# Two column groups by two token blocks in seven block products instead of eight, and four phases, in the second feed-forward network

## The chip, the cores and the metric

The kernel runs on one core of a Trainium2 chip. A core has engines that work at the same time, each through its own queue in order: TensorE (PE, matmuls; PEld are its weight loads), VectorE (DVE), ScalarE (ACT), GpSimd (POOL) and SyncE (SP), which here issues the DMAs. The metric is the device time of one execution in microseconds (us); 1 us is 1000 ns.

## The reference

```python
def reference(...):
    attn_out = _attn_ref(...)                     # 2 x 8 heads, 768 tokens, depth 64, a window of 128 and 4 sinks
    x = attn_out.transpose(0, 2, 1, 3).reshape(1536, 512)
    x = ((x @ w_a) * (x @ w_b)) @ w_out           # first network: d_ff 1536
    h = np.maximum(x @ w_in, 0.0)                 # second network: d_ff 2048
    return (h * h) @ w_out2
```

All of it is in float32. The change lies in `x @ w_in`, the second network's first product: 1536 tokens, depth 512, 2048 columns.

## The kernel before

**Data.** Activations lie with the depth on the 128 partitions: `xh` and `xl` hold four slices of depth by 1536 tokens. Each float32 number is split into a rounded high half and the rest (`split`, lines 59 and 60: ScalarE casts the high half, VectorE subtracts for the low half). A product takes three matmuls per slice of depth: high by high, high by low, low by high.

**Weights.** They come from DRAM as 64-bit words, in pieces of 128 x 512 numbers (a column group's first-product weights for all four slices of depth, or its second-product weights). SyncE loads a piece into one of three `wraw` buffers. `Weights.stages` decodes it: ScalarE takes the upper words (line 517), VectorE runs four operations (521, 522, 525, 528), ScalarE casts the high half `wh` (533), VectorE subtracts the low half `wl` (535). The two halves fill a slot; there are 14 slots `FIRST` and 9 more (`NSLOT`, pool `sb`) from the end of the attention. `ahead` is called at every beat of the network's program and decodes the next piece at every third beat (`PACE`) if a slot is free; `done` gives a phase's slots back after the last token block.

**Loops.** The tokens are three blocks of 512, the column groups have 128 columns. A network works in phases of a few column groups: the first in (4, 4) after four groups done beside the attention, the second in (5, 5, 6). In each phase `block` runs over the three token blocks. For a column group in the second network: `inner` (line 625) runs 12 matmuls of 128x512 into one PSUM bank `psa`; ScalarE takes relu (695), VectorE squares (705), `split` makes `gh` and `gl`, and `outer` (line 666) runs 12 matmuls with the second-product weights into four accumulators `acc`, one half before and one behind the next group's `inner`. At the end of a phase the accumulators are drained into `part` (copy, line 725, in the first phase; addition, line 727, in later ones), and in the last phase stored (731). In the last phase of the first network `part` is the network's result and is split into `xh` and `xl`. PSUM has four banks for `psa` (`ps_a`) and four for `acc` (`ps_y`).

**Order.** In the attention an order written out by hand holds on TensorE, VectorE, ScalarE and GpSimd. Behind it the scheduler of the Tile framework places the instructions of all engines, by its own estimates and by the program's order; it moves matmuls of neighbouring steps into each other.

Of the kernel before, what the change touches and what calls it, by code (L numbers as in the profile page):

```python
# [18 lines left out]
P = 128  # L19
SK = 8  # L20
AHEAD1 = 4
PHASES1 = (4, 4)
PHASES2 = (5, 5, 6)
FIRST, NSLOT = 14, 9
PACE = 3
NRAW, AHEAD = 3, 2
# [14 lines left out]
T = 512  # L41
# [414 lines left out]
class Weights:  # L456
# [7 lines left out]
    def __init__(self, tc, cp, rp, w_a, w_b, w_out, w_in2, w_out2):  # L464
        self.tc, self.rp = tc, rp
        self.n = 0
        FF1, FF2 = w_a.shape[0], w_in2.shape[0]

        def piece(w, f):
            return w.bitcast(I32)[f]  # L470


        f = AHEAD1
        self.phases = [[(piece(w_a, j), piece(w_b, j)) for j in range(f)]]
        for n in PHASES1:
            self.phases.append([(piece(w_a, j), piece(w_b, j), piece(w_out, j)) for j in range(f, f + n)])
            f += n
        assert f == FF1
        self.phases[1][0:0] = [(piece(w_out, j),) for j in range(AHEAD1)]
        f = 0  # L480
        for n in PHASES2:
            self.phases.append([(piece(w_in2, j), piece(w_out2, j)) for j in range(f, f + n)])
            f += n
        assert f == FF2
        self.todo = [(ph, f, j) for ph in range(len(self.phases)) for f in range(len(self.phases[ph]))
                     for j in range(len(self.phases[ph][f]))]
        self.order = list(self.todo)
# [17 lines left out]
    def stages(self, pin=False):  # L505

        while len(self.raws) < AHEAD and self.next < len(self.order):
            self.load()
        nc = self.tc.nc
        key = self.todo.pop(0)  # L510
        hi, lo = slot = self.free.pop(0)
        self.where[key] = slot
        raw = self.raws.pop(0)
        up, low = raw[:, :, 1], raw[:, :, 0]
        t = self.rp.tile([P, 512], I32, name="wtmp", tag="wtmp", bufs=3)
        tf = t.bitcast(F32)
        a = nc.scalar.activation(tf, up.bitcast(F32), AF.Abs)  # L517
# [12 lines left out]
        while len(self.raws) < AHEAD - 1 and self.next < len(self.order):  # L530
            self.load()
        yield
        nc.scalar.copy(hi, tf)  # L533
        yield
        nc.vector.tensor_sub(lo, tf, hi.bitcast(F32))  # L535
        yield

    def convert(self):

        if not self.todo or not self.free:  # L540
# [12 lines left out]
    def get(self, ph, f, j):  # L553
        while (ph, f, j) not in self.where:
            assert self.convert()
        return self.where[ph, f, j]

    def done(self, ph, f):

        for j in range(len(self.phases[ph][f])):  # L560
            self.free.append(self.where[ph, f, j])


class Beside:
# [43 lines left out]
class Ffn:  # L608


    def __init__(self, tc, W, xh, xl, gp, out):
        self.tc, self.W, self.xh, self.xl, self.gp, self.out = tc, W, xh, xl, gp, out

        self.gs = [gp.tile([P, AHEAD1, T], F32, name=f"gs{j}", tag=f"gs{j}") for j in range(xh.shape[2] // T)]
        self.part = {}

    def inner(self, ph, f, j, ts, ps_a):
        W, xh, xl = self.W, self.xh, self.xl
# [10 lines left out]
    def ahead(self, t0, last, ps_a, wk):  # L629


        nc = self.tc.nc
        ts = slice(t0, t0 + T)
        for f in range(AHEAD1):
            u = wk.tile([P, T], F32, name="u", tag="u")
            pa = self.inner(0, f, 0, ts, ps_a)
            yield "fu"
            nc.scalar.copy(u, pa)
            yield None
            pb = self.inner(0, f, 1, ts, ps_a)  # L640
# [4 lines left out]
            yield None  # L645

    def block(self, ph, t0, last, ps_y, ps_a, wk):

# [73 lines left out]
        for j, b_ in enumerate(acc):  # L722
            p_ = self.part[blk][:, j]
            if first:
                nc.scalar.copy(p_, b_)
            else:
                nc.vector.tensor_add(p_, p_, b_)
            if final and one:
                split(nc, xh[:, j, ts], xl[:, j, ts], p_)
            elif final:  # L730
                nc.sync.dma_start(self.out[t0 + j * P:t0 + (j + 1) * P, :], p_)
        yield
# [2 lines left out]
@with_exitstack  # L735
def sliding_window_moe_kernel(ctx, tc, q, k, v, vs, span, w_a, w_b, w_out, w_in2, w_out2, out):
    nc = tc.nc
    NT, DM = out.shape
    cp = ctx.enter_context(tc.tile_pool(name="cp", bufs=1))
    xp = ctx.enter_context(tc.tile_pool(name="xp", bufs=1))  # L740
    xh = xp.tile([P, DM // P, NT], F32R, name="xh")
    xl = xp.tile([P, DM // P, NT], F32R, name="xl")
    rp = ctx.enter_context(tc.tile_pool(name="rp", bufs=3))
    sa = ctx.enter_context(tc.tile_pool(name="sa", bufs=1))

    def slots(pool, n):
        return [(pool.tile([P, 512], F32R, name=f"wh{j}"), pool.tile([P, 512], F32R, name=f"wl{j}")) for j in range(n)]

    first = slots(sa, FIRST)
    zero = cp.tile([P, P], mybir.dt.bfloat16, name="zero")  # L750
    nc.vector.memset(zero, 0.0)
    mk = ctx.enter_context(ExitStack())
    tp = mk.enter_context(tc.tile_pool(name="mk", bufs=1, side="right"))
    c = setup(tc, cp, tp, span)

    def run(attend):
        W = Weights(tc, cp, rp, w_a, w_b, w_out, w_in2, w_out2)
        W.free = list(first)
        F = Ffn(tc, W, xh, xl, xp, out)
        with ExitStack() as c0:  # L760
            c0.callback(mk.close)
            wk0 = c0.enter_context(tc.tile_pool(name="wk0", bufs=2, side="right"))
            beside = Beside(tc, W, F, wk0, c0, zero, NT)
            with ExitStack() as c1, tc.manual_schedule(engines=ORDERED):
                attend(c1, beside)
            with tc.tile_pool(name="sb", bufs=1) as sb:
                W.free += slots(sb, NSLOT)
                for at in beside.work:
                    if at is None:
                        W.ahead()  # L770
                c0.close()
                with ExitStack() as c2:
                    ps_a = c2.enter_context(tc.tile_pool(name="ps_a", bufs=4, space=PSUM))
                    ps_y = c2.enter_context(tc.tile_pool(name="ps_y", bufs=4, space=PSUM))
                    wk = c2.enter_context(tc.tile_pool(name="wk", bufs=2))
                    for ph in range(1, len(W.phases)):
                        for t0 in range(0, NT, T):
                            for _ in F.block(ph, t0, t0 + T == NT, ps_y, ps_a, wk):
                                W.ahead()

    def attend_any(ctx, beside):
# [76 lines left out]
```

## Time and profile before

| what | value |
|---|---|
| time, median of 3 runs | 651.21 us (650.08 to 651.23) |
| the profiled execution's own time | 650.44 us |
| its span | 648.6 us |
| TensorE's granted clock, mean | 0.999 |
| instructions | 8803 |

The span goes from the first to the last instruction of the profiled execution; its own time also has what lies around that. A matmul's end is modelled, and its record overlaps the next one's, so counts and spacing say more than the sum of durations. The attention, with parts of the first network beside it, ends at about 126 us; the second network's first products begin among the last matmuls of the first network, and the first eviction of one (line 695) starts at 381.9 us.

### The profile page before, as it was taken

The page shows a single profiled execution, that of the slowest core. Times are in us where ns is not written, and L with a number is a line of the kernel's source. Part 1 is how long each engine was busy: PE and PEld are TensorE (multiplying, and loading weights), DVE is VectorE, ACT ScalarE, POOL GpSimd, SP SyncE. Part 2 cuts the span into 40 slices and gives each one's busy share as a digit, 9 for nine tenths or more (in the row PEclk, how much of TensorE's full clock was granted, in tenths as well). Part 3 has the DMA queues.
Part 4 walks back from the last instruction along what each step waited for, and adds up shares of the span by engine and source line. Part 5 has one row for each costly group of instructions (what it writes and reads, how often), then busy time and mean ns, then how long its engine had stood idle before and what let it go on. Part 6 is the DMA issues. An engine that isn't in the chain of part 4 may idle for free.

```text
span 648.6 us, 8803 instructions
## 1 busy us (share of the span) xinstructions
PE 636.6 (98%) x3206; PEld 515.5 (79%) x3206; DVE 385.7 (59%) x908; ACT 278.9 (43%) x652; POOL 56.2 (9%) x132
## 2 busy tenths in 40 slices
PE   9889999999999999999999999999999999999996
PEld 6567777887888888888888888888888888888885
DVE  6989988238889525997324998228624233232323
ACT  6898777425446225554213554326522222222221
POOL 2554354300000000000000000000000000000000
PEclk9999999999999999999999999999999999999999
DMA  8544422003444300444000243002000000010101
GB/s 295 193 134 138 168 82 74 2 33 116 144 163 162 131 0 33 158 164 165 1 1 9 89 162 114 17 0 71 28 1 1 1 1 0 1 48 18 44 23 70
DMA packets 17411, 49.47 MB, mean 76 GB/s; under 512 B 2064, under 2 KB 2576, under 8 KB 17360
## 3 DMA queue, kind: packets, MB, share of 16 engines
q1 hardware_dynamic: 17216, 48.83, 21.6%
q8 instruction: 27, 0.44, 0.3%
q14 instruction: 24, 0.20, 0.1%
q10 hardware_dynamic: 144, 0.00, 0.0%
HBM read 45.68 MB, written 3.15 MB: 75 GB/s over the span
## 4 chain that ended last, share of the span: by engine, by line
PE 93%; DVE 3%; ACT 1%; issue 1%; POOL 0%; POOLq 0%; ACTq 0%
PE psa L625 50%; PE acc L666 35%; PE x L325 3%; PE sc L226 3%; PE ptp L287 1%; PE x L330 1%; DVE ex L242 1%; ACT ex L250 1%; PE psw L352 0%; DVE wtmp L525 0%; ACT ex L265 0%; DVE wtmp L528 0%; DVE sc L239 0%; DVE wtmp L521 0%; PE pst L311 0%
## 5 line engine op out<-in xcount | busy, mean ns | idle before, releaser
L625 PE MATMUL psa<-xh,wh 128*128 128x512 f32 x480 | 188.2, 392 | 0.0
L625 PE MATMUL psa<-xh,wl 128*128 128x512 f32 x480 | 186.8, 390 | 0.0
L625 PE MATMUL psa<-xl,wh 128*128 128x512 f32 x480 | 186.8, 389 | 0.0
L625 PEld LDWEIGHTS psa<-xh,wl 128*128 128x128 f32 x480 | 90.1, 188 | 18.9
L625 PEld LDWEIGHTS psa<-xl,wh 128*128 128x128 f32 x480 | 90.2, 188 | 18.3
L625 PEld LDWEIGHTS psa<-xh,wh 128*128 128x128 f32 x480 | 90.1, 188 | 18.2
L705 DVE TENSOR_TENSOR g<-u 128x512 f32<-128x512 f32 x48 | 33.2, 691 | 112.4 <-ACT u L695 112.4
L695 ACT ACTIVATE u<-psa 128x512 f32<-128x512 f32 x48 | 28.7, 598 | 120.6 <-PE psa L625 120.5
L59 ACT CAST gh<-g 128x512 fp32r<-128x512 f32 x72 | 44.7, 621 | 69.9 <-DVE g L702 36.0
L666 PE MATMUL acc<-wh,gl 128*128 128x512 f32 x192 | 74.7, 389 | 0.0
L666 PE MATMUL acc<-wl,gh 128*128 128x512 f32 x192 | 74.7, 389 | 0.0
L60 DVE TENSOR_TENSOR gl<-g,gh 128x512 fp32r<-128x512 f32 x72 | 49.7, 690 | 31.8 <-ACT gh L59 31.6
L517 ACT ACTIVATE wtmp<-wraw 128x512 f32<-128x512 f32 x68 | 45.8, 676 | 47.1 <-DMA wraw<-in_moe_w_out_dram 9.9
L666 PE MATMUL acc<-wh,gh 128*128 128x512 f32 x192 | 62.7, 389 | 0.0
L535 DVE TENSOR_TENSOR wl<-wtmp,wh 128x512 fp32r<-128x512 f32 x68 | 47.4, 700 | 17.0 <-ACT wh L533 16.0
L533 ACT CAST wh<-wtmp 128x512 fp32r<-128x512 f32 x68 | 41.9, 619 | 36.0 <-DVE wtmp L528 15.7
L666 PE MATMUL acc<-gl,wh 128*128 128x512 f32 x144 | 56.1, 390 | 0.2 <-DVE gl L60 0.2
L666 PE MATMUL acc<-gh,wl 128*128 128x512 f32 x144 | 56.0, 389 | 0.0
L525 DVE SCALAR_TENSOR_TENSOR wtmp<-wraw,wtmp 128x512 int32<-128x512 int32 x68 | 47.0, 696 | 0.3
L666 PE MATMUL acc<-gh,wh 128*128 128x512 f32 x144 | 47.1, 389 | 0.0
L528 DVE SCALAR_TENSOR_TENSOR wtmp<-wraw,wtmp 128x512 int32<-128x512 int32 x68 | 46.3, 685 | 0.2
L666 PEld LDWEIGHTS acc<-wh,gh 128*128 128x128 f32 x192 | 36.0, 188 | 7.5
(83 smaller groups left out, 719.4 us busy)
## 6 DMA issues: line engine op xcount, KB each, us to landing
wraw<-in_moe_w_out_dram SPq DMA_DIRECT2D x28, 512.0 KB, 3.5
wraw<-in_moe_w_in_dram SPq DMA_DIRECT2D x16, 512.0 KB, 3.4
wraw<-in_moe_w_a_dram SPq DMA_DIRECT2D x12, 512.0 KB, 3.4
wraw<-in_moe_w_b_dram SPq DMA_DIRECT2D x12, 512.0 KB, 3.5
values<-in_v_dram SPq DMA_DIRECT2D x12, 256.0 KB, 4.1
out_dram<-part SPq DMA_DIRECT2D x12, 256.0 KB, 2.2
keys<-in_k_dram SPq DMA_DIRECT2D x11, 272.0 KB, 3.9
queries<-in_q_dram SPq DMA_DIRECT2D x11, 256.0 KB, 3.8
```

The source lines that it names most:

```text
L59: nc.scalar.copy(hi, src)
L60: (lo_eng or nc.vector).tensor_sub(lo, src, hi.bitcast(F32))
L226: nc.tensor.matmul(o, lhsT=half(queries[n], r)[:, 2 * m + pp], rhs=y, start=True, stop=True)
L517: a = nc.scalar.activation(tf, up.bitcast(F32), AF.Abs)
L525: nc.vector.scalar_tensor_tensor(out=t, in0=up, scalar=0x3FFFFFFF, in1=t, op0=ALU.bitwise_or, op1=ALU.bitwise_and)
L528: nc.vector.scalar_tensor_tensor(out=t, in0=low, scalar=29, in1=t, op0=ALU.logical_shift_right, op1=ALU.bitwise_or)
L533: nc.scalar.copy(hi, tf)
L535: nc.vector.tensor_sub(lo, tf, hi.bitcast(F32))
L625: self.tc.nc.tensor.matmul(ps, lhsT=w[:, kt, :], rhs=x[:, kt, ts], start=n == 0, stop=n == 3 * KT - 1)
L666: mm = nc.tensor.matmul(acc[d], lhsT=a, rhs=b_, start=f == 0 and j == 0, stop=f == NF - 1 and j == 2)
L695: nc.scalar.activation(u, pa, AF.Relu)
L705: nc.vector.tensor_mul(g, u, u)
```

## The change

The second network's first product is formed for two column groups (f, f + 1) and token blocks 0 and 1 together, in a unit. The two groups by the two halves of depth are a 2 x 2 matrix of weight blocks A, the halves of depth by the two token blocks one of activations B. Instead of eight block products (each two slices of depth, 6 matmuls) there are seven, in Winograd's form:

S1 = A21 + A22, S2 = S1 - A11, S3 = A11 - A21, S4 = A12 - S2; T1 = B12 - B11, T3 = B22 - B12, T2 = B22 - T1, T4 = B21 - T2.

C11 = A11 B11 + A12 B21. With V = A11 B11 + S2 T2 and Z = V + S3 T3: C21 = Z + A22 T4, C22 = Z + S1 T1, C12 = V + S1 T1 + S4 B22.

- `sum_x` makes the T of both slices once: 8 subtractions of 128x512 on GpSimd, in place of the `part` values of token blocks 0 and 1, each followed by a `split`; six slots taken out of the pool by `take` hold them, T1 lies in the place of B12 in `xh` and `xl`.
- `Weights.sums` makes the S of one pair: 4 GpSimd operations of 128x256 on the decoded words `wtmp` of the two pieces, then two splits into two slots. The order of a pair's pieces is now both first-product pieces, the sums, both second-product pieces; `order`, by which they are loaded, follows.
- `unit` runs the seven products. `px` keeps a running sum over five of them, which ScalarE copies out on the way; `py` has two products and `pz` one. The outputs of block 0 (C11, C21) are squared and split at once, those of block 1 are kept as squares in `ax` tiles until the accumulators of block 0 are drained. A relu and a square in one VectorE operation (line 738) take the place of two operations in three of the four outputs.
- `two` runs the two units of a phase and the second products of both blocks; block 2 runs through `block` as before.
- The phases are (4, 4, 4, 4). Nine slots become six, and three more (`early`) live only in phase 1; their room later holds the `ax` tiles.

```diff
-PHASES2 = (5, 5, 6)
+PHASES2 = (4, 4, 4, 4)
+NSUM, NAUX = 6, 3
...
+                self.todo += [(ph, f, 0), (ph, f + 1, 0), (ph, f, "sums"), (ph, f, 1), (ph, f + 1, 1)]
...
+    def sums(self, key, slot):
...
+        a11, a12, a21, a22 = a[:, 0:256], a[:, 256:512], b[:, 0:256], b[:, 256:512]
+        t, u = self.aux[0]
+        s1, s2, s3, s4 = t[:, 0:256], t[:, 256:512], u[:, 0:256], u[:, 256:512]
+        nc.gpsimd.tensor_add(s1, a21, a22)
+        nc.gpsimd.tensor_sub(s2, s1, a11)
+        nc.gpsimd.tensor_sub(s3, a11, a21)
+        nc.gpsimd.tensor_sub(s4, a12, s2)
+        yield
+        for (hi, lo), x in zip(two, (t, u)):
+            split(nc, hi, lo, x)
+        yield
...
+    def sum_x(self):
...
+        for k in range(2):
+            b11, b21, b12, b22 = b0[:, k], b0[:, 2 + k], b1[:, k], b1[:, 2 + k]
+            t1, t3, t2, t4 = b11, b12, b22, b21
+            nc.gpsimd.tensor_sub(t1, b12, b11)
+            nc.gpsimd.tensor_sub(t3, b22, b12)
+            nc.gpsimd.tensor_sub(t2, b22, t1)
+            nc.gpsimd.tensor_sub(t4, b21, t2)
+            self.sx[1, k] = xh[:, k, one], xl[:, k, one]
+            for n, t in ((1, t1), (3, t3), (2, t2), (4, t4)):
+                if n > 1:
+                    self.sx[n, k] = at.pop(0)
+                split(nc, *self.sx[n, k], t)
...
+    def unit(self, ph, f, ps_a, wk):
...
+        def add(ps, slot, n, xs, start):
+            for k in range(2):
+                hi, lo = w(slot, 2 * n + k)
+                bh, bl = xs(k)
+                for j, (a, b) in enumerate(((hi, bh), (hi, bl), (lo, bh))):
+                    nc.tensor.matmul(ps, lhsT=a, rhs=b, start=start and k == 0 and j == 0, stop=k == 1 and j == 2,
+                                     skip_group_check=True)
+
+        def square(c):
+            nc.vector.scalar_tensor_tensor(out=c, in0=c, scalar=0.0, in1=c, op0=ALU.max, op1=ALU.mult)
...
+        a0, a1 = W.get(ph, f, 0), W.get(ph, f + 1, 0)
+        sa, sb = W.get(ph, f, "sums")
+        c11 = wk.tile([P, T], F32, name="g", tag="g")
+        c12, c22 = W.aux[1 + f // 2]
+        px, py, pz = (ps_a.tile([P, T], F32, name=n, tag="ab") for n in ("px", "py", "pz"))
+        add(px, a0, 0, lambda k: x(k, first), True)
+        nc.scalar.copy(c11, px)
+        yield
+        add(pz, a0, 1, lambda k: x(2 + k, first), True)
+        nc.vector.tensor_add(c11, c11, pz)
+        square(c11)
+        yield (f, *halves(c11))
+        add(px, sa, 1, lambda k: self.sx[2, k], False)
+        nc.scalar.copy(c12, px)
+        yield
+        add(py, sa, 0, lambda k: self.sx[1, k], True)
+        yield
+        add(px, sb, 0, lambda k: self.sx[3, k], False)
+        nc.scalar.copy(c22, px)
+        nc.vector.tensor_add(c22, c22, py)
+        square(c22)
+        yield "fill"
+        add(px, a1, 1, lambda k: self.sx[4, k], False)
+        u = wk.tile([P, T], F32, name="u", tag="u")
+        nc.scalar.activation(u, px, AF.Relu)
+        nc.vector.tensor_mul(u, u, u)
+        yield "fill"
+        yield (f + 1, *halves(u))
+        add(py, sb, 1, lambda k: x(2 + k, one), False)
+        nc.vector.tensor_add(c12, c12, py)
+        square(c12)
+        self.later += [(f, c12), (f + 1, c22)]
+        W.done_sums(ph, f)
+        yield "fill"
+        yield "fill"
...
             if final and one:
-                split(nc, xh[:, j, ts], xl[:, j, ts], p_)
+                if blk != 1 or j > 1:
+                    split(nc, xh[:, j, ts], xl[:, j, ts], p_)
...
-                W.free += slots(sb, NSLOT)
+                W.free += slots(sb, NSLOT - NAUX)
...
                     for ph in range(1, len(W.phases)):
-                        for t0 in range(0, NT, T):
+                        if ph >= W.second:
+                            for _ in F.two(ph, ps_y, ps_a, wk):
+                                W.ahead()
+                        for t0 in range(2 * T if ph >= W.second else 0, NT, T):
                             for _ in F.block(ph, t0, t0 + T == NT, ps_y, ps_a, wk):
                                 W.ahead()
+                            if ph + 1 == W.second and t0 == T:
...
+                                F.sum_x()
```

Two places show how the order of the instructions moves. The first is TensorE between two column groups of the second network, whose matmuls the scheduler has moved into each other; `psa` is the bank of a group's first product, `wh` and `wl` are its weights, `acc` the second product's accumulators. Before:

```order
L625 MATMUL psa_4527<-xh_61,wh2_73 128x512
L625 MATMUL psa_4527<-xl_62,wh2_73 128x512
...
L666 MATMUL acc_4277<-wh8_1949,gh_4454 128x512
L666 MATMUL acc_4278<-wh8_1949,gh_4454 128x512
L666 MATMUL acc_4279<-wh8_1949,gh_4454 128x512
L666 MATMUL acc_4280<-wh8_1949,gh_4454 128x512
L625 MATMUL psa_4527<-xh_61,wl2_74 128x512
L625 MATMUL psa_4527<-xh_61,wh2_73 128x512
```

Of the change, the two units of the second of the four phases: `px_4321` and `px_4417` are their running banks; `wh0_69`, `wh3_1939`, `wh5_1943`, `wh2_1937` are slots that hold T3 and T2, `wh2_73` and `wh0_1933` hold weight sums.

```order
L734 MATMUL pz_4419<-xh_61,wl13_96 128x512
L734 MATMUL px_4321<-wh0_69,wh2_73 128x512
L734 MATMUL px_4321<-wl0_70,wh2_73 128x512
...
L734 MATMUL px_4321<-wh3_1939,wl2_74 128x512
L793 MATMUL acc_4316<-wh7_83,gh_4339 128x512
...
L793 MATMUL acc_4319<-wh7_83,gh_4339 128x512
L734 MATMUL px_4417<-wh5_1943,wh0_1933 128x512
...
L734 MATMUL px_4417<-wh2_1937,wl0_1934 128x512
L793 MATMUL acc_4316<-wh7_83,gl_4340 128x512
...
L793 MATMUL acc_4319<-wl7_84,gh_4339 128x512
L734 MATMUL px_4321<-wh4_1941,wh12_93 128x512
...
L734 MATMUL px_4321<-wh1_1935,wl12_94 128x512
```

Between two products of one `px` stand a product of the other unit's and second products; a group's twelve matmuls in one bank have become sixes in turn.

The second place is ScalarE in the passage from the first network to the second, from the splits of token block 1's result on; `u` are evictions of the first network's last column groups (token block 2), `part1_...` the result of token block 1. Before:

```order
L533 CAST wh1_71<-wtmp_3697 128x512
L693 COPY u_3615<-psa_3617 128x512
L517 ACTIVATE wtmp_3825<-wraw_3783 128x512
L59 CAST xh_61<-part1_2789 128x512 x2
L533 CAST wh2_73<-wtmp_3743 128x512
...
L533 CAST wh4_77<-wtmp_3825 128x512
L693 COPY u_3649<-psa_3651 128x512
L59 CAST gh_3645<-g_3616 128x512
```

Of the change (`wh0_69` to `wh1_1935` are the slots of the x sums, `wh4_77` and `wh5_79` hold pieces of weights):

```order
L60 CAST wh0_69<-part1_2792 128x512
L549 CAST wh4_77<-wtmp_3726 128x512
L884 COPY u_3592<-psa_3594 128x512
L60 CAST wh3_1939<-part1_2792 128x512
L60 CAST wh5_1943<-part1_2792 128x512
L549 CAST wh5_79<-wtmp_3766 128x512
L533 ACTIVATE wtmp_3809<-wraw_3764 128x512
L60 CAST wh2_1937<-part1_2792 128x512
L60 CAST gh_3628<-g_3593 128x512
L60 CAST wh4_1941<-part0_2475 128x512
L60 CAST wh1_1935<-part0_2475 128x512
```

Casts of x sums, which wait for GpSimd and VectorE, now stand in ScalarE's queue between the decoding of weights, the evictions and the casts `gh` of the first network's last block.

## Rows read from the trace of the kernel before

**Rows 1.** The page, part 1: busy us, share, instructions of each engine.

```profile
PE 636.6 (98%) x3206; PEld 515.5 (79%) x3206; DVE 385.7 (59%) x908; ACT 278.9 (43%) x652; POOL 56.2 (9%) x132
```

**Rows 2.** The page, part 4: the chain that ended last, by engine, by line.

```profile
PE 93%; DVE 3%; ACT 1%; issue 1%; POOL 0%; POOLq 0%; ACTq 0%
PE psa L625 50%; PE acc L666 35%; PE x L325 3%; PE sc L226 3%; PE ptp L287 1%; PE x L330 1%; DVE ex L242 1%; ACT ex L250 1%; PE psw L352 0%; DVE wtmp L525 0%; ACT ex L265 0%; DVE wtmp L528 0%; DVE sc L239 0%; DVE wtmp L521 0%; PE pst L311 0%
```

**Rows 3.** All of TensorE's waits: us in total, times, longest us.

```profile
PE pst L311 <- POOL sp L281: 4.5, 6, 1.0
PE psw L352 <- DVE zero L751: 1.0, 1, 1.0
PE sc L226 <- DVE nb L242: 0.2, 1, 0.2
PE acc L666 <- DVE gl L60: 0.2, 1, 0.2
```

**Rows 4.** Windows: length, busy (count) PE, PEld, DVE, ACT, POOL; PEclk, DMA, GB/s.

```profile
206.00:398.50 192.50, 192.50 (x851) 159.40 (x850) 126.96 (x232) 78.94 (x135) 0.00 (x0) 1.00 0.24 85
398.50:634.50 236.00, 236.00 (x1043) 195.42 (x1042) 91.87 (x146) 66.94 (x113) 0.00 (x0) 1.00 0.06 23
...
354.00:406.00 52.00, 52.00 (x231) 43.06 (x230) 47.55 (x88) 26.80 (x46) 0.00 (x0) 1.00 0.34 121
```

**Rows 5.** The page, part 5: one group of first-product matmuls.

```profile
L625 PE MATMUL psa<-xh,wh 128*128 128x512 f32 x480 | 188.2, 392 | 0.0
```

**Rows 6.** The chain in order of time: start us, us, what; two pieces.

```profile
128.04 21.85 PE psa L625 x96
...
248.09 10.88 PE acc L666 x48
```

**Rows 7.** Timeline of VectorE: start, us, engine, line, operation; three in a row.

```profile
216.00 0.68 DVE L60 TENSOR_TENSOR gl<-g,gh 128x512 fp32r<-128x512 f32 x1
216.60 0.42 DVE L521 TENSOR_SCALAR wtmp<-wtmp 128x512 f32<-128x512 f32 x1
216.94 0.68 DVE L528 SCALAR_TENSOR_TENSOR wtmp<-wraw,wtmp 128x512 int32<-128x512 int32 x1
```

**Rows 8.** ScalarE's groups by line: busy, mean ns, idle before.

```profile
L59 ACT CAST gh<-g 128x512 fp32r<-128x512 f32 x72 | 44.7, 621 | 69.9 <-DVE g L702 36.0 <-DVE g L705 33.8
...
L695 ACT ACTIVATE u<-psa 128x512 f32<-128x512 f32 x48 | 28.7, 598 | 120.6 <-PE psa L625 120.5
...
L725 ACT COPY part<-acc 128x512 f32<-128x512 f32 x24 | 12.6, 595 | 10.0 <-PE acc L666 10.0
```

**Rows 9.** GpSimd's elementwise forms: ns min/median/max; the last from its groups.

```profile
L279 POOL TENSOR_TENSOR ex<-ex,ss x20: 238/238/241, 13.2 to 118.0; 128x32 f32<-128x32 f32 x20
...
L304 POOL TENSOR_SCALAR_AFFINE_SELECT lu<-th x20: 634/635/1085, 19.9 to 125.2; 128x512 f32<-128x512 f32 x20
...
masks.py:199 POOL TENSOR_SCALAR_AFFINE_SELECT ident<-ident 128x128 f32<-128x128 f32 x1 | 0.3, 292 | 0.0
```

**Rows 10.** Timeline of GpSimd and VectorE in the attention, operations that overlap.

```profile
76.29 0.64 POOL L304 TENSOR_SCALAR_AFFINE_SELECT lu<-th 128x512 f32<-128x512 f32 x1
...
76.68 0.80 DVE L525 SCALAR_TENSOR_TENSOR wtmp<-wraw,wtmp 128x512 int32<-128x512 int32 x1
...
86.32 0.64 POOL L302 TENSOR_SCALAR_AFFINE_SELECT lu<-th 128x512 f32<-128x512 f32 x1 [1.25 <-ACT th L291]
...
86.34 0.90 DVE L522 TENSOR_SCALAR wtmp<-wtmp 128x512 int32<-128x512 int32 x1
...
98.63 1.08 POOL L304 TENSOR_SCALAR_AFFINE_SELECT lu<-th 128x512 f32<-128x512 f32 x1
```

**Rows 11.** The page, part 6: DMA loads, KB each, us to landing.

```profile
wraw<-in_moe_w_in_dram SPq DMA_DIRECT2D x16, 512.0 KB, 3.4
```

**Rows 12.** Timeline of the end: the last matmul and the last addition.

```profile
642.33 0.39 PE L666 MATMUL acc<-wl,gh 128*128 128x512 f32 x1
642.76 0.69 DVE L727 TENSOR_TENSOR part<-part,acc 128x512 f32<-128x512 f32 x1 [0.67 <-PE acc L666]
```

More of the change, by code (lines that the diff above doesn't have):

```diff
@@ L486, in __init__ @@
                      for j in range(len(self.phases[ph][f]))]
-        self.order = list(self.todo)
+        second = 1 + len(PHASES1)
+        self.todo = [key for key in self.todo if key[0] < second]
+        for ph in range(second, len(self.phases)):
+            for f in range(0, len(self.phases[ph]), 2):
+                self.todo += [(ph, f, 0), (ph, f + 1, 0), (ph, f, "sums"), (ph, f, 1), (ph, f + 1, 1)]
+        self.second = second
+        self.order = [key for key in self.todo if key[2] != "sums"]
+        self.kept = []
+        self.keep = NSUM
+        self.early, self.gone = [], []
         self.next = 0
@@ L510, in stages @@
         key = self.todo.pop(0)
-        hi, lo = slot = self.free.pop(0)
+        early = key[0] == 1 and self.early
+        hi, lo = slot = (early or self.free).pop(0)
         self.where[key] = slot
+        if key[2] == "sums":
+            yield from self.sums(key, slot)
+            return
         raw = self.raws.pop(0)
@@ L516, in stages @@
         tf = t.bitcast(F32)
+        if key[0] >= self.second and key[2] == 0:
+            self.kept.append(tf)
         a = nc.scalar.activation(tf, up.bitcast(F32), AF.Abs)
@@ L536, in stages, with take @@
         yield
-    def convert(self):
-        if not self.todo or not self.free:
+    def sums(self, key, slot):
+        nc = self.tc.nc
+        two = [slot, self.free.pop(0)]
+        self.where[key] = two
+        a, b = self.kept
+        self.kept = []
+        a11, a12, a21, a22 = a[:, 0:256], a[:, 256:512], b[:, 0:256], b[:, 256:512]
[9 more added lines that the diff above has]
+        yield
+    def take(self):
+        assert len(self.free) >= self.keep
+        got = [self.free.pop() for _ in range(self.keep)]
+        self.keep = 0
+        return got
+    def convert(self):
+        if not self.todo:
+            return False
+        ph, _, j = self.todo[0]
+        if ph == 1 and self.early:
+            pass
+        elif len(self.free) < (2 if j == "sums" else 1) + (self.keep if ph >= self.second else 0):
             return False
@@ L556, in get, with done_sums @@
         return self.where[ph, f, j]
+    def done_sums(self, ph, f):
+        self.free += self.where[ph, f, "sums"]
     def done(self, ph, f):
         for j in range(len(self.phases[ph][f])):
-            self.free.append(self.where[ph, f, j])
+            slot = self.where[ph, f, j]
+            (self.early if any(slot is x for x in self.gone) else self.free).append(slot)
 class Beside:
@@ L615, in __init__ @@
         self.part = {}
+        self.made = []
     def inner(self, ph, f, j, ts, ps_a):
@@ L645, in ahead @@
             yield None
+    def sum_x(self):
+        nc, xh, xl = self.tc.nc, self.xh, self.xl
+        at = self.W.take()
+        (b0, b1), one = (self.part[i] for i in range(2)), slice(T, 2 * T)
+        self.sx = {}
+        for k in range(2):
[10 more added lines that the diff above has]
+                split(nc, *self.sx[n, k], t)
@@ new lines, in unit, with x, w, halves @@
+    def unit(self, ph, f, ps_a, wk):
+        nc, W, xh, xl = self.tc.nc, self.W, self.xh, self.xl
+        first, one = slice(0, T), slice(T, 2 * T)
+        def x(k, ts):
+            return xh[:, k, ts], xl[:, k, ts]
+        def w(slot, k):
+            return [t[:, k * P:(k + 1) * P] for t in slot]
+        def add(ps, slot, n, xs, start):
[7 more added lines that the diff above has]
+            nc.vector.scalar_tensor_tensor(out=c, in0=c, scalar=0.0, in1=c, op0=ALU.max, op1=ALU.mult)
+        def halves(g):
+            gh = wk.tile([P, T], F32R, name="gh", tag="gh", bufs=3)
+            gl = wk.tile([P, T], F32R, name="gl", tag="gl", bufs=3)
+            split(nc, gh, gl, g)
+            return gh, gl
+        a0, a1 = W.get(ph, f, 0), W.get(ph, f + 1, 0)
[33 more added lines that the diff above has]
+        yield "fill"
@@ new lines, in outers, with outer, drain @@
+    def outers(self, ph, t0, last, ps_y):
+        nc, W = self.tc.nc, self.W
+        NF, DM = len(W.phases[ph]), self.xh.shape[1] * P
+        acc = [ps_y.tile([P, DM], F32, name="acc", tag="y") for _ in range(T // P)]
+        def outer(f, gh, gl, half):
+            oh, ol = W.get(ph, f, 1)
+            for d in range(2 * half, 2 * half + 2):
+                ds = slice(d * P, (d + 1) * P)
+                for j, (g_, w) in enumerate(((gh, oh), (gl, oh), (gh, ol))):
+                    nc.tensor.matmul(acc[d], lhsT=g_[:, ds], rhs=w, start=f == 0 and j == 0, stop=f == NF - 1 and j == 2)
+            if last and half == 1:
+                W.done(ph, f)
+        def drain():
+            for j, b_ in enumerate(acc):
+                p_ = self.part[t0 // T][:, j]
+                if ph == W.second:
+                    nc.scalar.copy(p_, b_)
+                else:
+                    nc.vector.tensor_add(p_, p_, b_)
+                if ph == len(W.phases) - 1:
+                    nc.sync.dma_start(self.out[t0 + j * P:t0 + (j + 1) * P, :], p_)
+        return outer, drain
@@ new lines, in two @@
+    def two(self, ph, ps_y, ps_a, wk):
+        nc, NF = self.tc.nc, len(self.W.phases[ph])
+        outer, drain = self.outers(ph, 0, False, ps_y)
+        self.later, pend = [], []
+        for f in range(0, NF, 2):
+            for at in self.unit(ph, f, ps_a, wk):
+                if at == "fill" and pend:
+                    outer(*pend.pop(0))
+                elif at not in (None, "fill"):
+                    self.made.append(at)
+                yield
+            pend += [(*g, h) for g in self.made for h in range(2)]
+            self.made = []
+        for p_ in pend:
+            outer(*p_)
+            yield
+        drain()
+        outer, drain = self.outers(ph, T, False, ps_y)
+        for f, g in sorted(self.later, key=lambda x: x[0]):
+            gh = wk.tile([P, T], F32R, name="gh", tag="gh", bufs=3)
+            gl = wk.tile([P, T], F32R, name="gl", tag="gl", bufs=3)
+            split(nc, gh, gl, g)
+            for h in range(2):
+                outer(f, gh, gl, h)
+                yield
+        drain()
+        yield
@@ L775, in run @@
                     wk = c2.enter_context(tc.tile_pool(name="wk", bufs=2))
+                    c3 = c2.enter_context(ExitStack())
+                    W.early += slots(c3.enter_context(tc.tile_pool(name="se", bufs=1)), NAUX)
+                    W.gone = list(W.early)
                     for ph in range(1, len(W.phases)):
-                        for t0 in range(0, NT, T):
+                        if ph >= W.second:
+                            for _ in F.two(ph, ps_y, ps_a, wk):
+                                W.ahead()
+                        for t0 in range(2 * T if ph >= W.second else 0, NT, T):
                             for _ in F.block(ph, t0, t0 + T == NT, ps_y, ps_a, wk):
                                 W.ahead()
+                            if ph + 1 == W.second and t0 == T:
+                                assert len(W.early) == NAUX
+                                c3.close()
+                                ax = c2.enter_context(tc.tile_pool(name="ax", bufs=1))
+                                W.aux = [[ax.tile([P, T], F32, name=f"ax{i}{j}") for j in range(2)] for i in range(NAUX)]
+                                F.sum_x()
     def attend_any(ctx, beside):
```

## Prediction

> **What bounds the kernel now.** I read the busy times first, then the chain of waits, then TensorE's own waits, then the stages. The page gives TensorE 98% of a span of 648.6 us, VectorE 59%, ScalarE 43%, GpSimd 9% [rows 1]. The chain that ended last lies 93% on TensorE, and its two large parts are the first products (line 625, 50%) and the second products (line 666, 35%) [rows 2]. TensorE's own waits add up to 5.9 us in the whole run, 5.7 of them in the attention and at the very start; in the feed-forward stages one wait of 0.2 us is left [rows 3]. By stage: from 206 us to 634.5 us TensorE is busy for every microsecond of every window, at a granted clock of 1.00, the upper of its two levels (2.4 GHz) [rows 4]. So in the second network the time is the number of matmuls times their spacing, and everything else is hidden. That is the stage that the change touches.
>
> **The spacing.** A 128x512 matmul's record lasts 0.39 us [rows 5], but they overlap; the chain gives 48 in 10.88 us and 96 in 21.85 us [rows 6], so 0.2267 us each. The term uses that and not 0.39.
>
> **What it removes.** For a pair of column groups and the first two token blocks the first product was 8 block products of 6 matmuls (two slices of depth, three terms of the split). Now it is 7. Eight pairs by 6 is 48 matmuls; the order of TensorE shows exactly 48 fewer and none of another shape. 48 x 0.2267 = 10.88 us, all on the path. The second products, the third token block and the first network keep their matmuls.
>
> **What it adds**, counted in the order of instructions:
> - VectorE: 58 operations on 128x512 (16 for the low halves of weight sums, 6 for those of x sums, 12 drains for the fourth phase, 24 in place of squares done as one step). Back to back one costs 0.60 us and the two-scalar form 0.34 us [rows 7]. 58 x 0.60 = 35 us.
> - ScalarE: 22 more operations of about 0.6 us [rows 8], 13 us.
> - GpSimd: 32 two-tensor sums of 128x256 and 8 of 128x512. Rows of before show neither size.
> - No DMA: the same 123 rows on SyncE, the first-product pieces of a pair now loaded before its second-product pieces.
>
> From 206 us to 634.5 us VectorE is busy 127 + 92 = 219 of 428.5 us and ScalarE 146 [rows 4]. 35 and 13 us fit there many times over as sums; what counts is whether they stand in front of something that TensorE waits for. Three places decide.
>
> **First, the hand-overs inside a unit.** One PSUM bank, px, takes five of the seven products, and ScalarE copies the running sum out four times between them, so TensorE gets four new waits per unit, 32 in all. An eviction takes 0.6 us [rows 8], and it can start 0.39 us after its last matmul's start. With 0.1 us for signals that is 1.1 us. The order shows the cover: between px's last matmul and its next one stand 12 matmuls in the tightest place (2.7 us) and 15 to 27 in the others. So I take nothing. Without cover it would be 32 x 1.1 = 35 us; a tenth of that is my bound upward, 3.5 us. Queued behind such a waiting matmul on TensorE are the next products, which nothing else can replace.
>
> **Second, the passage from the first network to the second.** There the x sums, two weight sums, decoding, the last block of the first network and two units come together. Between the matmul after which block 1 is drained and the last first-unit addition that TensorE waits for, the order puts 81 VectorE operations (64 of the long kind, 17 of the two-scalar kind) beside 227 matmuls. 64 x 0.60 + 17 x 0.34 = 44.2 us against 227 x 0.2267 = 51.5 us: 7 us free. Before is no emptier: in its stretch from 354 to 406 us VectorE ran 88 operations and TensorE was busy 52.00 of 52.00 us [rows 4]. New is that VectorE and ScalarE, which work in order, wait there for GpSimd.
>
> **Third, the price of GpSimd's sums.** The one two-tensor form in the trace, 128x32, takes 0.238 us. The select with one input takes 0.292 us on 128x128 and 0.635 us on 128x512: 0.18 us fixed and 0.9 ns per element. With two inputs at twice the slope, 128x32 would be 0.24 us, which is what the row shows; so I take 0.18 + 1.8 ns per element: 1.1 us on 128x512 and 0.64 us on 128x256 [rows 9]. Lower end: the one-input select, 0.635 us for 512. Upper end: the 128x32 row scaled straight, 16 x 0.238 = 3.8 us, and 1.9 us for 256. At 1.1 us the eight x sums take 9 us from the first drain. Line by line: ScalarE's conversion of the activation for matmul group 2 of the third block stands behind the sixth sum's result, ready at 6 x 1.1 + 1.2 = 7.8 us; TensorE asks 63 matmuls later, at 14.3 us. 6 us free. A weight sum (four steps, 2.6 us) stands in front of the next decode on ScalarE, and behind that the evictions of a unit; the tightest place leaves 9.3 us from the second piece's decode to the matmul that needs the eviction. Nothing is late, so nothing is added. The Trainium skill (GPSIMD Engine Reference, Engine selection) speaks against such sums: elementwise work with two inputs is about twice as slow there as on VectorE, 4497 ns at 2048 elements. An estimate from that page is 1.1 us for 512 elements, close to the value above; the sum would be the same.
>
> **Contention.** While GpSimd's selects ran, VectorE's long operation took 0.80 instead of 0.68 us and the two-scalar form 0.90 instead of 0.42, and one select took 1.08 instead of 0.64 us [rows 10]. In the passage 8 x 1.1 + 8 x 0.64 = 13.9 us of GpSimd meet VectorE. If one fifth is lost, that is 2.5 us of the 7 free. I charge 0.5 us for the passage, since VectorE also waits for others there.
>
> **DMA.** A piece lands 3.4 us after its issue [rows 11]; three buffers are in turn, and in the passage a decode takes about 5 us of VectorE's queue, so the loads stay hidden. In the first network six slots fewer may be decoded ahead, but the order of TensorE there differs only within a block, and three splits of stored activations move ahead of a decode. The 0.2 us wait may go; I take zero.
>
> **The end.** Behind the last group of token block 2 the order is as before: 18 matmuls after the first accumulator is complete, one VectorE addition of 0.69 us starting 0.43 us after the last matmul's start [rows 12], the same stores. Zero.
>
> **Sum.** The profiled execution took 650.44 us for its span of 648.6. 650.44 - 10.88 + 0.5 = 640.1 us. The median of the three runs, 651.21, lies 0.8 above the profiled one, their lowest, 650.08, 0.4 below.
>
> **Rivals.**
> A. VectorE and GpSimd shut each other out in the passage. For: [rows 10], and most VectorE operations there read two SBUF tensors. Against: the long form lost only 0.12 us beside a select of 0.64. Full exclusion gives 44.2 + 13.9 = 58.1 us against 51.5: TensorE 6.6 us late, 646.2 us. The Trainium skill (Advanced Engine Details and Errata, VectorE Performance Modes) says that the second Vector SBUF port is shared with GpSimd and that the two block each other. Its rule in full would give this rival; the trace agrees for the two-scalar form, by [rows 10], and in part for the other.
> B. Hand-overs of px are not all covered, because ScalarE's queue holds a decode or a split in front of an eviction. For: in-order queues with 22 operations more. Against: 12 to 27 matmuls of cover. At the bound, 3.5 us: 643.6 us.
> C. Slower than before: GpSimd's sums cost the straight-scaled 3.8 and 1.9 us. Then the sixth x sum is ready at 22.8 + 1.2 us where TensorE asks at 14.3: 9.7 us late. The eighth sum (30.4 us) holds the next eviction, about 3 us more, and the weight sums of 7.6 us each exceed their room in the passage, 2 us. 639.6 + 14.7 = 654 us. It decides from about 3.3 us per x sum, where the loss passes 10.9. For: no row of that size. Against: the fixed part in the select's two rows, which a straight scaling counts sixteen times.
> D. The change gives nothing that can be told, since A, B and a part of C add up: 650 us.
>
> **Chances.** Forecast 0.72, A in part or in full 0.12, B 0.09, C 0.04, D 0.03. What a measurement of this kernel can tell from no change is about 0.2%, 1.3 us. Forecast, A and B are all faster by more: 0.93; D 0.03; C 0.04. The range starts at 638.6 us (the lowest run less 10.88, and the 0.2 us wait gone, is 639.0, and another 0.4, the distance of the lowest run from the profiled one) and goes to 644.5, which takes in B and the first part of A.
>
> **What would show it.** Right: 48 matmuls fewer at 0.227 us, no TensorE wait above 0.3 us after 150 us, windows from 206 us on fully busy, GpSimd's 128x512 sum at 1.0 to 1.5 us. A shows as VectorE operations above 0.9 us and TensorE waits on VectorE at about 355 to 400 us; B as waits of px's matmuls on ScalarE; C as GpSimd sums above 3 us and ScalarE waiting for them. The forecast is wrong if TensorE's busy time falls by 10.9 us and the span does not.

## The result and the profile after

The changed kernel takes 645.04 us (median of 4 runs, 644.47 to 645.19) against 650.64 us before (the three runs told of above and one more): a ratio of 0.9913, 95% interval 0.9896 to 0.9930. It is faster, but by 5.6 us and not by the 10.5 that were forecast, and 645.04 lies 0.5 us above the range. The profiled execution has a span of 643.0 us.

The busy times of the changed kernel (the page's first part), which answer to [rows 1]:

```profile
PE 628.8 (98%) x3158; PEld 508.0 (79%) x3158; DVE 432.0 (67%) x966; ACT 288.9 (45%) x674; POOL 99.1 (15%) x172
```

The counts are those forecast: 48 matmuls fewer, VectorE 58, ScalarE 22 and GpSimd 40 operations more. GpSimd's busy time has grown by 43 us where the estimate was 9 + 8 x 2.6 = 30.

TensorE's waits in the changed kernel, all of them (us in total, times, longest), for [rows 3]:

```profile
PE pst L312 <- POOL sp L282: 4.3, 6, 1.0
PE acc L857 <- ACT gh L60: 2.0, 1, 2.0
PE psw L353 <- DVE zero L943: 1.0, 1, 1.0
PE px L734 <- ACT ax L759: 0.7, 1, 0.7
```

Two are new: 2.0 us in `acc` and 0.7 us in `px`. The windows of the changed kernel (columns as in [rows 4]) tell where; the second fence looks closer at the first stop:

```profile
340.00:380.00 40.00, 38.04 (x161) 31.00 (x161) 29.89 (x37) 16.41 (x29) 16.68 (x12) 0.96 0.05 15
380.00:400.00 20.00, 19.32 (x85) 15.35 (x84) 19.97 (x38) 11.81 (x21) 4.21 (x4) 1.00 0.38 131
400.00:440.00 40.00, 40.00 (x178) 33.14 (x177) 33.07 (x56) 21.21 (x38) 4.10 (x4) 1.00 0.24 79
440.00:630.00 190.00, 190.00 (x840) 157.34 (x839) 124.91 (x209) 68.29 (x117) 13.82 (x16) 1.00 0.13 45
```

```profile
366.00:368.50 2.50, 0.72 (x4) 0.26 (x2) 2.50 (x4) 1.67 (x3) 0.23 (x1) 1.00 0.00 0
368.50:372.50 4.00, 3.81 (x10) 3.00 (x11) 4.00 (x9) 2.17 (x5) 0.00 (x0) 0.57 0.00 0
```

From 400 us on TensorE is full. Everything that is missing went between 366 and 397 us, in the passage. The first stop cost more than its wait: behind it the granted clock was 0.57 of full over 4 us, most of it at 0.50, the lower level of 1.2 GHz. TensorE's timeline there (start, us, engine, line, operation):

```profile
366.34 0.39 PE L677 MATMUL psa<-xh,wl 128*128 128x512 f32 x1
368.69 1.07 PE L857 MATMUL acc<-gh,wh 128*128 128x512 f32 x2 [1.96 <-ACT gh L60]
369.55 0.63 PE L677 MATMUL psa<-xh,wh 128*128 128x512 f32 x1
369.98 0.63 PE L677 MATMUL psa<-xl,wh 128*128 128x512 f32 x1
...
372.44 0.39 PE L857 MATMUL acc<-gl,wh 128*128 128x512 f32 x1
372.66 0.39 PE L857 MATMUL acc<-gh,wl 128*128 128x512 f32 x1
```

From 366.34 to 372.66 lie 11 matmuls; at 0.2267 us they need 2.5 us and took 6.32: 3.8 us lost, 2.1 of them by standing and 1.7 by the clock. The second stop, counted in the same way from 394.65 to 397.26 us, lost 1.25. Together 5.1 us.

Behind the first stop stands VectorE. Its timeline in the changed kernel, and GpSimd's x sums (lines 708 to 711):

```profile
352.03 2.48 DVE L918 TENSOR_TENSOR part<-part,acc 128x512 f32<-128x512 f32 x4 [1.82 <-PE acc L857]
354.59 0.69 DVE L893 TENSOR_TENSOR g<-u,psa 128x512 f32<-128x512 f32 x1
355.20 2.48 DVE L61 TENSOR_TENSOR xl<-part,xh 128x512 fp32r<-128x512 f32 x2
357.60 1.78 DVE L61 TENSOR_TENSOR wl<-ax,wh 128x512 fp32r<-128x512 f32 x1
...
365.00 1.78 DVE L551 TENSOR_TENSOR wl<-wtmp,wh 128x512 fp32r<-128x512 f32 x1
366.70 0.68 DVE L61 TENSOR_TENSOR wl<-part,wh 128x512 fp32r<-128x512 f32 x1
367.30 0.68 DVE L893 TENSOR_TENSOR g<-u,psa 128x512 f32<-128x512 f32 x1
```

```profile
352.86 2.56 POOL L708 TENSOR_TENSOR part<-part,part 128x512 f32<-128x512 f32 x2 [81.70 <-DVE part L918]
355.38 3.45 POOL L709 TENSOR_TENSOR part<-part 128x512 f32<-128x512 f32 x2
358.80 1.73 POOL L710 TENSOR_TENSOR part<-part,part 128x512 f32<-128x512 f32 x1
361.22 1.61 POOL L710 TENSOR_TENSOR part<-part,part 128x512 f32<-128x512 f32 x1 [0.69 <-DVE xl L61]
362.79 3.44 POOL L711 TENSOR_TENSOR part<-part,part 128x512 f32<-128x512 f32 x2
```

While GpSimd works on its sums, a VectorE operation with two SBUF operands takes 1.78 us instead of the 0.68 of [rows 7], and the next one starts 1.70 us later. At 366.2 us GpSimd is done, and VectorE is back at 0.68 at once. The operations with an operand in PSUM (`acc`, `psa`) are not slowed, and the sums beside them take 1.3 us and not 1.7. At 367.30 us the product `g` starts, which the cast `gh` needs, for which TensorE stands.

The second stop lies on ScalarE, whose queue works in order. A cast waits for a weight sum of GpSimd, and the copy out of `px` stands behind it:

```profile
395.01 0.62 ACT L60 CAST wh<-ax 128x512 fp32r<-128x512 f32 x1 [1.78 <-POOL ax L565]
396.06 0.57 ACT L759 COPY ax<-px 128x512 f32<-128x512 f32 x1
396.69 0.50 PE L734 MATMUL px<-wh,wh 128*128 128x512 f32 x1 [0.68 <-ACT ax L759]
```

### The profile page after: what moved, and what is told of

Read it like the earlier page. It is cut to its first block, busy times and chain, and to the rows that moved or that the text cites. A ratio compares the mean times of both kernels' runs of the same rounds, so it can differ in the third digit from the quotient of the medians.

```text
span 643.0 us, 8835 instructions
## 1 busy us (share of the span) xinstructions
PE 628.8 (98%) x3158; PEld 508.0 (79%) x3158; DVE 432.0 (67%) x966; ACT 288.9 (45%) x674; POOL 99.1 (15%) x172
## 4 chain that ended last, share of the span: by engine, by line
PE 88%; DVE 7%; issue 1%; ACT 1%; POOL 1%; POOLq 0%
PE psa L677 35%; PE acc L857 20%; PE acc L793 13%; PE px L734 6%; PE sc L227 3%; PE py L734 3%; PE x L326 3%; PE ptp L288 1%; PE pz L734 1%; PE psw L353 1%; PE x L331 1%; DVE xl L61 1%; DVE wl L61 1%; DVE wtmp L541 1%; DVE wl L551 1%
## 5 line engine op out<-in xcount | busy, mean ns | idle before, releaser
L677 PE MATMUL psa<-xh,wh 128*128 128x512 f32 x352 | 138.9, 395 | 0.0
L677 PE MATMUL psa<-xh,wl 128*128 128x512 f32 x352 | 137.7, 391 | 0.0
L677 PE MATMUL psa<-xl,wh 128*128 128x512 f32 x352 | 137.5, 391 | 0.0
L677 PEld LDWEIGHTS psa<-xh,wl 128*128 128x128 f32 x352 | 66.4, 189 | 14.1
L677 PEld LDWEIGHTS psa<-xl,wh 128*128 128x128 f32 x352 | 66.4, 189 | 13.4
L677 PEld LDWEIGHTS psa<-xh,wh 128*128 128x128 f32 x352 | 66.4, 189 | 13.2
L793 PE MATMUL acc<-wh,gl 128*128 128x512 f32 x128 | 49.8, 389 | 0.0
L793 PE MATMUL acc<-wl,gh 128*128 128x512 f32 x128 | 49.5, 389 | 0.0
L793 PE MATMUL acc<-wh,gh 128*128 128x512 f32 x128 | 43.7, 390 | 0.0
L537 DVE TENSOR_SCALAR wtmp<-wtmp 128x512 f32<-128x512 f32 x68 | 30.6, 453 | 18.5 <-ACT wtmp L533 18.1
```

Of the source, the lines that this page charges most:

```text
L677: self.tc.nc.tensor.matmul(ps, lhsT=w[:, kt, :], rhs=x[:, kt, ts], start=n == 0, stop=n == 3 * KT - 1)
L793: nc.tensor.matmul(acc[d], lhsT=g_[:, ds], rhs=w, start=f == 0 and j == 0, stop=f == NF - 1 and j == 2)
```

## The experiments

Each run's median has in it where the attention ended, which differed by up to 1 us between the profiled runs: its last matmul (line 331 or 330) starts at 127.2 to 128.2 us, in the kernel before at 127.60 and not at about 126. The last column leaves that out: the time from that matmul's start to the start of the last matmul, both read from the timeline. Each ratio is against runs of the kernel before that were taken beside it (medians of 650.44 to 650.90 us).

| kernel | median us | ratio to before, 95% | attention's last to last matmul, us |
|---|---|---|---|
| before | 650.64 | | 514.73 |
| changed | 645.04 | 0.9913 (0.9896 to 0.9930) | 508.42 |
| x sums on VectorE (e1) | 638.75 | 0.9818 (0.9801 to 0.9834) | 503.33 |
| all sums on VectorE (e3) | 639.72 | 0.9830 (0.9814 to 0.9847) | 503.32 |
| no x sums (e5) | 638.93 | 0.9822 (0.9805 to 0.9838) | 503.33 |
| weight sums on VectorE (e2) | 642.61 | 0.9883 (0.9867 to 0.9900) | 506.26 |
| e1 and 8 idle sums on GpSimd (e7) | 646.03 | 0.9935 (0.9918 to 0.9951) | 509.77 |
| e1 and 8 idle one-input operations (e9) | 640.65 | 0.9842 (0.9826 to 0.9859) | 504.71 |
| one-input operations for x sums (e6) | 640.66 | 0.9850 (0.9833 to 0.9866) | 504.25 |
| e1 and the eighth product (e8) | 650.92 | 1.0007 (0.9997 to 1.0016) | 514.85 |
| before, in four phases (e4) | 650.93 | 1.0002 (0.9992 to 1.0011) | 514.71 |

My theory was that GpSimd's x sums slow VectorE (E). The rivals: VectorE's queue is too full, whoever adds (Q), the phases cost (P), the sums' results come late (L).

**e1: x sums on VectorE.**

```diff
-            nc.gpsimd.tensor_sub(t1, b12, b11)
+            nc.vector.tensor_sub(t1, b12, b11)
```

(and so for t3, t2, t4)

> The 8 x sums of 128x512 run on VectorE instead of GpSimd; the weight sums stay on GpSimd. Theory E (exclusion: while GpSimd adds two SBUF tensors, a VectorE operation with two SBUF tensors takes 1.77 instead of 0.69 us, so VectorE's queue falls behind in the passage): VectorE gets 8 x 0.60 = 4.8 us more, but its two-tensor operations between 352 and 368 us go back to 0.69 us; the TensorE wait of 2.0 us and the low clock behind it (3.8 us together) go, the later stop of 1.2 us at px stays: 641.2 us. Rival Q (VectorE's queue in the passage is too full, whoever makes the sums): 4.8 us more in it make the TensorE wait longer, 645 to 650 us.

638.75 us. TensorE's waits in this kernel, and the stretch of VectorE that was slow, as a window of the changed kernel and of this one:

```profile
PE pst L312 <- POOL sp L282: 4.4, 6, 1.0
PE psw L353 <- DVE zero L943: 1.0, 1, 1.0
PE sc L227 <- DMA queries<-in_q_dram: 0.3, 1, 0.3
```

```profile
352.86:366.23 13.37, 13.37 (x61) 11.07 (x60) 13.29 (x12) 6.61 (x12) 12.67 (x8) 1.00 0.01 2
```

```profile
352.00:366.00 14.00, 14.00 (x63) 11.63 (x62) 14.00 (x25) 9.54 (x17) 0.00 (x0) 1.00 0.01 2
```

VectorE has the eight sums more to do and gets through 25 operations in 14.0 us, where it did 12 in 13.4. Both columns of busy time read about 100%: a held operation counts as busy, so the share doesn't show the loss, the count does. No wait is left behind the attention. Q is refuted. The 641.2 us expected were too much by 2.5: the second stop (1.25 us) went too, and the attention ended 1.0 us earlier than in the changed kernel.

**e5: no x sums.** The four lines of `sum_x` that subtract are taken out.

> The x sums are left out (the splits that follow read the unsummed tiles; this part of the computation is missing), nothing else is changed: VectorE and ScalarE have the same operations, GpSimd 8 fewer. Theory E: VectorE at 0.69 us in the passage, the 3.8 us go, the stop at px by the weight sums stays: 641.2 us. Rival Q: VectorE's queue is as full as before, 645 us.

638.93 us, the same as with the sums on VectorE, and again without the second stop, which was expected to stay. On VectorE the sums cost nothing that can be measured, on GpSimd 5.1 us (508.42 against 503.33).

**e3: all sums on VectorE**, the four lines of `sums` as well.

> x sums and weight sums all on VectorE, GpSimd does nothing after the attention. Theory E: no contention anywhere; VectorE gets 4.8 us and 32 x 0.35 = 11 us more, of which about 7.5 us in the passage; both stops go: 640 us, with VectorE at 0.69 us per two-tensor operation. Rival Q: VectorE in the passage is 7.5 us over, 648 us or more.

639.72 us; counted from the attention's end it equals e1 to 0.01 us. The 32 weight sums on GpSimd cost nothing in e1, though VectorE's two-tensor operations beside them took up to 1.23 us there: no matmul waited for them.

**e2: weight sums on VectorE, x sums on GpSimd.**

> x sums on GpSimd as in the changed kernel, weight sums on VectorE. Theory E: the x sums alone make the first stop (3.8 us); the second one (1.2 us), where ScalarE stood behind a cast that waited for a weight sum, goes: 641 to 643.5 us. If the second stop was only an echo of the first, weight sums on either engine make no difference, 645 us.

642.61 us. The first stop stands as in the changed kernel:

```profile
365.80 0.39 PE L677 MATMUL psa<-xh,wl 128*128 128x512 f32 x1
368.15 0.73 PE L857 MATMUL acc<-gh,wh 128*128 128x512 f32 x2 [1.96 <-ACT gh L60]
368.71 0.39 PE L677 MATMUL psa<-xh,wh 128*128 128x512 f32 x1
```

The x sums alone make it. But no low clock follows it: the matmuls are 0.23 us apart from 368.71 on. Of the second stop some 0.6 us are left. Neither the x sums here nor the weight sums in e1 make all of the second stop by themselves; that it was the delay of both together is an inference from these two runs.

**e7: nobody waits for the sums.** To e1 are added 8 subtractions on GpSimd whose results nobody reads.

```diff
+        for i in range(8):
+            nc.gpsimd.tensor_sub(self.W.aux[1 + i // 4][i // 2 % 2], xh[:, 2, one].bitcast(F32), xl[:, 2, one].bitcast(F32))
```

> The kernel with the x sums on VectorE (638.75 us), and beside them 8 more two-tensor subtractions of 128x512 on GpSimd at the same place, whose results nobody reads (they use xh and xl of token block 1). Theory E (VectorE is held back while GpSimd works on two SBUF tensors): VectorE's two-tensor operations take 1.7 us again in the passage, its queue has 4.8 us more than in the changed kernel, so TensorE stops for 4 to 8 us: 643 to 647 us. Rival L (the loss came from results of GpSimd that were late, not from a slower VectorE): nothing waits for these sums, 638.8 us.

646.03 us, 7.3 us more than e1. TensorE, VectorE and ScalarE have the same instructions in the same order in both, so nothing but the eight GpSimd operations differs. VectorE in this kernel, and the GpSimd line (ns min/median/max):

```profile
362.31 0.68 DVE L895 TENSOR_TENSOR g<-u,psa 128x512 f32<-128x512 f32 x1
362.91 1.19 DVE L551 TENSOR_TENSOR wl<-wtmp,wh 128x512 fp32r<-128x512 f32 x1
364.02 1.77 DVE L61 TENSOR_TENSOR wl<-part,wh 128x512 fp32r<-128x512 f32 x1
365.72 1.78 DVE L712 TENSOR_TENSOR part<-part,part 128x512 f32<-128x512 f32 x1
367.42 1.51 DVE L537 TENSOR_SCALAR wtmp<-wtmp 128x512 f32<-128x512 f32 x1
```

```profile
L706 POOL TENSOR_TENSOR ax<-xh,xl x8: 1469/1736/5292, 358.3 to 373.4; 128x512 f32<-128x512 f32 x8
```

Nor did the eight push back the weight sums behind them in GpSimd's queue: between the last of the eight and the first weight sum GpSimd stood idle for 5.8 us, until VectorE had decoded the weights. L is refuted, and E shown: the loss comes from GpSimd's work on SBUF, not from its results.

**e9 and e6: one input.** In e9 the eight idle operations are `tensor_scalar_mul(..., 0.5)`; in e6 those take the place of the x sums in the changed kernel.

> As the run with 8 idle two-tensor subtractions on GpSimd beside the x sums on VectorE, but each of the 8 is a multiplication with a constant, one input, 128x512; the instructions of TensorE, VectorE and ScalarE stand in the same order in both. Theory E2 (what holds VectorE back is mostly that GpSimd reads two tensors): VectorE's two-tensor operations at 0.7 to 1.1 us, a loss of 0 to 2 us against 638.75: 638.8 to 640.8 us. Rival E1 (any GpSimd operation of that length holds VectorE back alike): 1.7 us per operation and about 645 us.

> The changed kernel with the 8 x sums on GpSimd replaced by 8 multiplications with a constant, 128x512, one input each (the sums are missing from the computation). Theory E with the exclusion only between two-input operations: VectorE at 0.7 to 0.8 us as beside the selects in the attention, 639 to 640.5 us. If every GpSimd operation shuts VectorE out alike, the loss of 5 us is in proportion to their length. Rival L: it depends only on when they end; at 1.3 to 1.7 us each, 645 us as before.

640.65 and 640.66 us. The GpSimd line of e9, and VectorE beside it:

```profile
L706 POOL TENSOR_SCALAR ax<-xh x8: 1487/1648/1700, 355.1 to 366.1; 128x512 f32<-128x512 f32 x8
```

```profile
361.68 1.09 DVE L551 TENSOR_TENSOR wl<-wtmp,wh 128x512 fp32r<-128x512 f32 x1
362.69 0.68 DVE L61 TENSOR_TENSOR wl<-part,wh 128x512 fp32r<-128x512 f32 x1
363.29 1.09 DVE L712 TENSOR_TENSOR part<-part,part 128x512 f32<-128x512 f32 x1
364.31 0.67 DVE L895 TENSOR_TENSOR g<-u,psa 128x512 f32<-128x512 f32 x1
364.90 0.94 DVE L551 TENSOR_TENSOR wl<-wtmp,wh 128x512 fp32r<-128x512 f32 x1
```

One input holds VectorE back by 0.4 us per GpSimd operation, two inputs by 1.1. The records are of nearly the same length (1.65 against 1.74 us), but a record has GpSimd's own waiting in it (one of e7's eight lasted 5.29 us): in e9 one lasts about as long as two VectorE operations (starts 1.0 and 0.6 us apart), in e7 as long as one (1.7 us). What such an operation takes alone no row shows, and the two differ in their kind of instruction as well as in the number of inputs, so which of these decides is not shown. The order of the instructions is again that of e1. Counted from the attention's end the eight one-input operations cost 1.4 us, the eight sums 6.4. Of the 1.4, one stop at `px` makes 1.1: ScalarE's copy stands behind a decode that waited 0.74 us for its load. In e1 a decode waited there for 0.79 us too, and no matmul stood. E1 is refuted in e9, L in e6, which came out 0.2 us above the range of E.

**e8: the eighth product back.** In e1 the line `add(pz, a0, 1, ...)` stands twice.

> The kernel with the x sums on VectorE (638.75 us), and in each unit the six matmuls of one product (A12 B21 into pz) run twice, the second time over the first: 48 matmuls more, nothing else. Price of the 48 removed matmuls as predicted: 48 x 0.2267 = 10.9 us, so 649.6 us. If part of the 48 was hidden behind other waits, less.

650.92 us, 1.3 above the 649.6 expected. From the attention's end it is 11.5 us more than e1; the timeline shows one stop at `px` of 0.6 us (0.3 of it a wait for ScalarE's copy, line 760), and 11.5 - 0.6 = 10.9 is the price forecast. The rest is the attention, which ended 0.8 us later than in e1.

**e4: four phases alone.**

> The kernel before with the second network's phases (4, 4, 4, 4) in place of (5, 5, 6), eight products as before. Theory E and Q: 12 more drains on VectorE, hidden: 650.6 us, within 0.2 per cent. Rival P (the division into four phases costs by itself, for instance by later weights at a phase's start): 653 us or more, and then a part of the missing 5 us is the phases'.

650.93 us, and 514.71 against 514.73 us from the attention's end: the division costs nothing that can be measured, P is refuted.

## Why the prediction was wrong

- **The 48 matmuls**: right, 10.9 us by e8.
- **The wait of 0.2 us in [rows 3], taken as zero**: it went, and that gave 0.5 us. In the trace of before seven matmuls lie between 155.16 and 157.24 us, which need 1.6 us and took 2.1: the wait and the slower spacing just behind it.
- **Phases, DMA, the end**: right. The changed kernel has no wait of TensorE for a load, and the last matmul starts 6.37 us before the end of the span, against 648.6 - 642.33 = 6.27.
- **The hand-overs of px**: nearly right where nothing is held back: e1, e3 and e5 have no wait there, e8 one of 0.3 us. The one of 0.7 us in the changed kernel was ScalarE's copy (line 759) behind a cast that stood for a weight sum of GpSimd, which is the place that rival B named. The 0.1 us for signals, for which the prediction names no row, comes out of the rows: 0.04 us from the end of a matmul's record to the operation that waits for it ([rows 12]) and 0.06 from a copy's end to its matmul (396.63 to 396.69 us in the changed kernel).
- **GpSimd's price**: 1.1 us assumed per x sum; measured 1.30 beside VectorE operations on PSUM, 1.74 beside others. The sixth sum was ready 10.0 us after the first began instead of 6.6. No matmul stood for that: ScalarE waited 1.1 us for x sums in all, and right after it 5.1 us for VectorE.
- **Contention: the step that failed.** It said: "If one fifth is lost, that is 2.5 us of the 7 free. I charge 0.5 us". Two parts of it were wrong. The loss: one fifth of 13.9 us would be 2.8; measured, each of the six sums that ran beside VectorE operations with two SBUF operands held VectorE for 1.1 us, 6.6 in all, so it did 12 operations in 13.4 us where 25 in 14.0 are possible. And the room: the 7 us free were an average over 51.5 us of passage and by that sum would have hidden even this, but the loss falls into its first 14 us. The product `g` started at 367.30 us; in e1 it starts at 361.88. The loss on the path was 5.1 us and not 0.5, so 11.4 (10.88 and the 0.5 above) less 5.1 is the 6.3 us that the table shows.
- **What misled me** was [rows 10]. The 0.12 us lost there were lost beside a select, which has one input, and the two overlapped for 0.25 us only (76.68 to 76.93). The trace of before has no two-input operation of that size on GpSimd, but it has a VectorE operation with two SBUF operands that overlapped with selects for its whole length, and that took 1.12 us instead of 0.68:

```profile
54.20 1.12 DVE L535 TENSOR_TENSOR wl<-wtmp,wh 128x512 fp32r<-128x512 f32 x1
```

```profile
53.80 0.97 POOL L302 TENSOR_SCALAR_AFFINE_SELECT lu<-th 128x512 f32<-128x512 f32 x1
54.73 1.08 POOL L304 TENSOR_SCALAR_AFFINE_SELECT lu<-th 128x512 f32<-128x512 f32 x1
```

- **Rival A** was the right one: it named the mechanism and the place, and it had 0.12. Its 646.2 us against 645.04 is close in part by luck. It set 13.9 us of full exclusion against the mean room of the whole passage; measured, 6.6 us beside the x sums were lost early in it, and 1.7 us of the time came from a low clock that it didn't have.
- The rule that I quoted beside rival A stands in the Trainium skill (Advanced Engine Details and Errata, VectorE Performance Modes): the second Vector SBUF port is shared with GpSimd, so that GpSimd's instructions and VectorE's 2p ones block each other. My quotation left out the 2p. e7 shows such blocking for operations that merely have two SBUF operands, 1.77 against 0.68 us, which that sentence doesn't name.
- **The low clock behind a stop** was in no term. It made 1.7 of the 5.1 us.

The version with the x sums on VectorE beats both kernels: 638.75 us, 12 us under the kernel before, with no TensorE wait behind the attention.

## What to carry to other kernels

In this kernel an idle GpSimd was no free help for a busy VectorE: a sum of two SBUF operands took more of VectorE's time there (1.1 us) than VectorE needs for it itself (0.6 us). Such work cost nothing where VectorE had room, as the weight sums of e1, and took nothing from VectorE while its operations read PSUM. And free time in a queue is to be counted up to the first moment that somebody waits for it, not as a mean over a stage.

## What the runs showed of the hardware

- A GpSimd operation with two SBUF inputs and a VectorE one with two SBUF operands took turns, one each: starts 1.70 us apart on VectorE, about 0.6 + 1.1. In e7 VectorE first ran on at 0.60 us spacing while one GpSimd operation took 5.29 us (358.26 to 363.55); then the turns began. That operation ended 1.24 us after VectorE had started one with an operand in PSUM (362.31), about the length of a sum beside such operations (1.3); that GpSimd got its turn by it is not shown.
- VectorE's single-input form was held as well (1.51 us instead of 0.42 in e7), one with an operand in PSUM wasn't (0.68).
- Three stops of TensorE of 2.1 us, each after it had been busy throughout from 340 us on, were followed by different clocks. In the changed kernel the granted clock was 0.50 from 369 to 372 us; behind the stop of e2 and that of e7 (from 371.7 to 374.1 us) it was 1.00. What decides it the runs don't settle.
